# Moving the second quarter's sets of batch 0 behind the first feature tile

## The chip, the core and the metric

The kernel runs on one core of a Trainium2 chip. The metric is the device time of one execution in microseconds (us), as the median of several runs. Times inside an execution come from a hardware profile of one of them, counted from the start of its span.

The engines are TensorE (PE in the profile's rows; PEld is its weight loads), VectorE (DVE), ScalarE (ACT), GpSimd (POOL, which does nothing here) and SyncE (SP), which issues the loads from memory.

## The reference

Two things are computed in a row. First a two-way attention between 8 x 8 heads of 512 tokens and 32 state rows; then every row (tokens and state rows, 4608 of them with 512 columns) goes through a bilinear layer in float32:

```python
a = x @ w1            # 512 -> 1024
b = x @ w2
h = a * b @ w3        # 1024 -> 1024
return h @ w_out      # 1024 -> 512
```

The attention's token side is `softmax(x @ state.T / 8) @ state` per head, its state side is `softmax(state @ x.T / 8) @ x`. The weights are float64 and reach the chip as their bits.

## The kernel before

**Algebra.** The kernel multiplies `w3 @ w_out` once (`w34`, kept as `wo`, split into a high and a low part). A token's attention output is its softmax row times the state, so for every batch the kernel multiplies the state into `w1` and `w2` first (the "sets", tiles `sw_hi` and `sw_lo`), and the softmax rows (`at_hi`, `at_lo`) are then multiplied with these sets. A product of float32 accuracy is three products of rounded parts (hi x hi, hi x lo, lo x hi).

**Feature tiles.** The 1024 hidden columns are 8 feature tiles of 128. `stage1(b, ft)` (called `stage1_sums` and `hidden`) does one: 12 TensorE instructions at line 344 into a PSUM buffer of two banks, a copy by ScalarE (L325), a product by VectorE (L326), and a split into `g_hi` (ScalarE, L99) and `g_lo` (VectorE, L100). There are three two-bank buffers (`ps_2`), shared by feature tiles and sets, each free again after its last reader. Single banks (`ps_o`, two of them) serve the `w34` products.

**Weights.** `w1` and `w2` come in eight pieces of 128 x 1024 (`convert_half(n)`, n = 0 to 7): piece 2q is quarter q of `w1`, piece 2q + 1 the same of `w2`. Converting float64 bits takes, for each piece, a load of 1 MB by SyncE (L116) into one of three `raw` buffers, two ScalarE activates (L120 for the high words, L130 for the low words into one of two `ulps` buffers), then on VectorE a shift (L134) and an add (L138) into `w_sb`. `to_f32` is a generator: the first `go` on it issues the load and the two activates, the second `go` the shift and the add; `run` issues all of it.

**Sets.** `sets(quarter)` makes the sets of one quarter of the hidden columns for batch 0: two units (`w1` and `w2`), each 16 TensorE instructions (L151) into a PSUM buffer, and a split by ScalarE (L99) and VectorE (L100). Quarter q needs pieces 2q and 2q + 1; feature tiles 2q and 2q + 1 read its columns. Quarters 2 and 3 are made together by `sw_steps(0)[2:]`, two units that need pieces 4 and 6, and 5 and 7.

**The last w3 column tiles.** `w34(i)` makes row block i of `wo`: 8 products, 16 TensorE instructions at L635, into a single bank; `finish(i)` splits it into `wo` (L99, L100). `w34(7)` was cut in two: products 0 to 4 (`LAST = 5`) ahead of `sets(1)`, 5 to 7 behind it.

**What sets the order.** TensorE and SyncE run in the order written, throughout. ScalarE and VectorE do so in the prologue, until `order.close()` (L701). After it a planner orders their instructions by priority among those that it takes to be ready; it may also put such later instructions between or ahead of the written ones while those wait. `tc.high_priority()` in `hidden` raises a feature tile's evacuation. `tc.issue_after(ins)` keeps instructions of a block behind `ins` on its engine.

Around the change the order written is: `w34(6)`, `sets(0)`, `finish(6)`, five products of `w34(7)`, `sets(1)`, three products, `finish(7)`, end of the written order; then for quarter 0 feature tiles 0 and 1, the conversions of pieces 4 to 7, and batch 1's load (`load_x(1)`); for quarter 1 feature tile 2, `sw_steps(0)[2:]`, the first output products (`early_stage2(0)`, L358), feature tile 3, and so on.

Of the kernel before, what the change touches and what calls it, by code (L numbers as in the profile page):

```python
# [30 lines left out]
NF = 512  # L31
NW = 1024
AHEAD = 2
LAST = 5
PARTS = {0: (640, 1024), 1: (512, 1024)}
WARM = 15
PLAIN = 1
# [3 lines left out]
def attn_bilinear_kernel(  # L41
# [16 lines left out]
    FT, DO = w34_k.shape[0], out.shape[2]  # L58
    HALF = FT * P // NF
    QT = 2 * HALF  # L60
    NQ = NF // 2
# [28 lines left out]
    def bank():  # L90
        return ps_o.tile([P, NF], F32, name="ps_o")

    def two_banks():
        return ps_2.tile([P, 2, NF], F32, name="ps_2")

    def split(hi, lo, src):

        return (
            nc.scalar.copy(out=hi, in_=src),  # L99
            nc.vector.tensor_tensor(out=lo, in0=src, in1=hi.bitcast(F32), op=ALU.subtract),  # L100
        )
# [43 lines left out]
    def per_head(ps, b, moving):  # L145


        for j in range(NP):
            for q in range(KT):
                rows = slice(q * D, (q + 1) * D)  # L150
                nc.tensor.matmul(  # L151
                    ps[j * NS:(j + 1) * NS, q], sts[b][rows, j], moving(rows, j), start=True, stop=True
                )

    def load_x(b):
        sts[b] = att.tile([P, NP, NS], F32, name="st")
        nc.sync.dma_start(out=sts[b], in_=st[b])
        x_tiles[b] = att.tile([P, NP, S], F32, name="x_d", bufs=1)
        nc.sync.dma_start(out=x_tiles[b], in_=x_d[b])
# [132 lines left out]
        return scores, read_state, a2  # L292


    def sw_pair():
        return [main.tile([P, KT, NF], F32R, name=f"sw_{part}", bufs=2 * HALF) for part in ("hi", "lo")]

    def sw_steps(b):
        sw_tiles.setdefault(b, {})

        def unit(half, i):
            ps = two_banks()
            as_q = ps.rearrange("p k (c f) -> p k c f", c=2)
            per_head(as_q, b, lambda rows, j: w_sb[rows, 2 * half:2 * half + 2, i, j])
            sw_tiles[b][half, i] = sw_pair()
            split(*sw_tiles[b][half, i], ps)

        return [(lambda half=half, i=i: unit(half, i)) for half in range(HALF) for i in range(2)]

    def sw_quarter(b, quarter, i):  # L310
        tiles = sw_tiles.setdefault(b, {})
        half, c = divmod(quarter, 2)
        if c == 0:
            tiles[half, i] = sw_pair()
        ps = two_banks()[:, :, :NQ]
        per_head(ps, b, lambda rows, j: w_sb[rows, quarter, i, j])
        split(*(t[:, :, c * NQ:(c + 1) * NQ] for t in tiles[half, i]), ps)


    last_split, stored = [], []  # L320

    def hidden(ps, n, g_hi, g_lo):
        a_sb = main.tile([P, NF], F32, name="tmp", bufs=4)
        with tc.high_priority():
            nc.scalar.copy(out=a_sb[:, :n], in_=ps[:, 0, :n])  # L325
            nc.vector.tensor_tensor(out=a_sb[:, :n], in0=a_sb[:, :n], in1=ps[:, 1, :n], op=ALU.mult)  # L326
            last_split[:] = split(g_hi, g_lo, a_sb[:, :n])

    def new_g(ft):
        if ft < FT - 2:  # L330
            return [main.tile([P, NF], F32R, name=f"g_{part}", bufs=FT - 2) for part in ("hi", "lo")]
        both = main.tile([P, 2, NF], F32R, name="g_x", bufs=2)
        return [both[:, 0], both[:, 1]]

    def stage1_sums(b, ft):
        half, c = divmod(ft * P, NF)
        ps = two_banks()
        hi, lo = at_tiles[b]
        for i in range(2):
            w_hi, w_lo = sw_tiles[b][half, i]  # L340
            k = 0
            for kt in range(KT):
                for w, a in ((w_hi, lo), (w_hi, hi), (w_lo, hi)):
                    nc.tensor.matmul(  # L344
                        ps[:, i], w[:, kt, c:c + P], a[:, kt], start=(k == 0), stop=(k == 3 * KT - 1)
                    )
                    k += 1
        return ps

    def stage1(b, ft, gs):  # L350
        ps = stage1_sums(b, ft)
        gs.append(new_g(ft))
        hidden(ps, S, *gs[-1])
# [23 lines left out]
    def side_steps():  # L377

        scores, reads[1], _ = attention_steps(1)
        w = sw_steps(1)  # L380
        softmax, read = scores(), reads[0]()

        def rest():

            with tc.issue_after(stored[0].ins):
                yield from softmax
            yield from read

        loads = [partial(load_tokens, 1), partial(load_x, 2)]
        late_units[:] = w[3:]  # L390
        return [[partial(islice, softmax, 3)], [partial(islice, read, 1), *loads, *w[:3]], [rest], [], [], []]
# [4 lines left out]
    def combine_weights(k):  # L396

        raw = [tmp_tile() for _ in range(2)]
        for i, whole in enumerate(raw):
            nc.vector.tensor_tensor(  # L400
                out=whole, in0=wo["hi"][:, i * QF + k].bitcast(F32), in1=wo["lo"][:, i * QF + k].bitcast(F32), op=ALU.add
            )
        b11, b12, b21, b22 = (whole[:, half * HO:(half + 1) * HO] for whole in raw for half in range(2))
        t = late.tile([P, QF, S], F32, name="raw")[:, :, :HO]
        for j, (x, y) in enumerate(((b12, b11), (b22, t[:, 0]), (b22, b12), (b21, t[:, 1]))):
            nc.vector.tensor_tensor(out=t[:, j], in0=x, in1=y, op=ALU.subtract)
        yield
        split(t_parts["hi"][:, :, k], t_parts["lo"][:, :, k], t)
# [163 lines left out]
    def run(steps):  # L572
        for step in steps:
            for _ in step() or ():
                pass
# [11 lines left out]
    def finish(i):  # L587
        split(wo["hi"][:, i], wo["lo"][:, i], w34_ps[i][:, :DO])
# [7 lines left out]
    def split_of(k):  # L596

        def both():
            halves[k] = sw_pair()
            for n, src in enumerate((w_out[k], chunks[k][:, DO:])):  # L600
                split(*(t[:, n] for t in halves[k]), src)

        return both
# [27 lines left out]
    def w34(i, ks=range(FT)):  # L631
        if ks[0] == 0:
            w34_ps[i] = bank()
        for k in ks:
            nc.tensor.matmul(  # L635
                w34_ps[i][:, :DO], w3s[i][:, k * P:(k + 1) * P], w_out[k], start=(k == 0), stop=(k == FT - 1)
            )
# [5 lines left out]
    def sets(quarter):  # L643
        for i in range(2):
            sw_quarter(0, quarter, i)


    gs, acc, early = [], [], range(2)

    def early_stage2(quarter):  # L650
        if quarter == 0:
            acc.extend(bank() for _ in early)
        for ft in range(2 * quarter, 2 * quarter + 2):
            for tt in early:
                project(acc[tt], gs, tt, ft)
# [19 lines left out]
    go = lambda steps: next(steps, None)  # L675
# [18 lines left out]
    w34(6)  # L694
    sets(0)
    finish(6)
    w34(7, range(LAST))
    sets(1)
    w34(7, range(LAST, FT))
    finish(7)  # L700
    order.close()  # L701
    for quarter in range(QT):
        stage1(0, 2 * quarter, gs)
        if quarter == 1:
            run(sw_steps(0)[2:])
        if quarter:
            early_stage2(quarter - 1)
        if quarter == 1:
            side = side_steps()
            sums = combine_weights(0)  # L710
            go(sums)
        elif quarter == 2:
            run(side.pop(0))
        stage1(0, 2 * quarter + 1, gs)
        if quarter == 1:
            with tc.issue_after(last_split[0].ins), tc.issue_after(last_split[1].ins):
                go(sums)
        if quarter == 0:
            run([partial(convert_half, n) for n in range(4, 2 * QT)])
            load_x(1)  # L720
            prologue.close()
            late = ctx.enter_context(tc.tile_pool(name="late", bufs=1))
            t_both = late.tile([P, 4, QF, 2, HO], F32R, name="t")
            t_parts = {part: t_both[:, :, :, n] for n, part in enumerate(("hi", "lo"))}
            with tc.issue_after(last_split[1].ins):
                go(softmax)
# [91 lines left out]
```

## Time and profile before

| | us |
|---|---|
| median of 3 runs (488.54 to 489.65) | 488.63 |
| the profiled execution | 487.95 |
| its span | 486.2 |
| TensorE busy | 479.5 |
| VectorE busy | 393.4 |
| ScalarE busy | 237.6 |
| span until the first feature tile of batch 0 starts | 65.7 |

Busy time of an engine leaves out waits, branches and the issue of loads. Matmuls are pipelined and their ends are modelled. A bracket at the end of a row gives the idle time of the engine just before the instruction and what ended it. The granted TensorE clock was 1.00 throughout.

### The profile page before, as it was taken

The page shows a single profiled execution, that of the slowest core. Times are in us where ns is not written, and L with a number is a line of the kernel's source. Part 1 is how long each engine was busy: PE and PEld are TensorE (multiplying, and loading weights), DVE is VectorE, ACT ScalarE, POOL GpSimd, SP SyncE. Part 2 cuts the span into 40 slices and gives each one's busy share as a digit, 9 for nine tenths or more (in the row PEclk, how much of TensorE's full clock was granted, in tenths as well). Part 3 has the DMA queues.
Part 4 walks back from the last instruction along what each step waited for, and adds up shares of the span by engine and source line. Part 5 has one row for each costly group of instructions (what it writes and reads, how often), then busy time and mean ns, then how long its engine had stood idle before and what let it go on. Part 6 is the DMA issues. An engine that isn't in the chain of part 4 may idle for free.

```text
span 486.2 us, 8627 instructions
## 1 busy us (share of the span) xinstructions
PE 479.5 (99%) x3398; PEld 370.2 (76%) x3398; DVE 393.4 (81%) x580; ACT 237.6 (49%) x368; POOL 0.2 (0%) x4
## 2 busy tenths in 40 slices
PE   8999999999999999999999999999999999999996
PEld 5554467768788878887797779777977797899885
DVE  5778999798899589959985998599859985678870
ACT  4876984453547045605560555055515642353640
POOL 0000000000000000000000000000000000000000
PEclk9999999999999999999999999999999999999999
DMA  8996971163014404130413042304230223001101
GB/s 345 367 399 222 388 278 26 19 216 89 14 38 173 106 4 182 38 93 4 182 41 92 5 181 45 87 5 181 47 84 6 89 47 85 5 2 45 45 1 43
DMA packets 56361, 52.49 MB, mean 108 GB/s; under 512 B 42752, under 2 KB 50944, under 8 KB 51712
## 3 DMA queue, kind: packets, MB, share of 16 engines
q1 hardware_dynamic: 47488, 43.27, 26.8%
q10 hardware_dynamic: 8832, 8.65, 5.2%
q8 instruction: 27, 0.44, 0.4%
q14 instruction: 14, 0.11, 0.1%
HBM read 38.27 MB, written 8.91 MB: 97 GB/s over the span
## 4 chain that ended last, share of the span: by engine, by line
PE 93%; DVE 4%; ACT 1%; DMA 1%; issue 0%; DVEq 0%; ACTq 0%
PE ps L344 36%; PE ps_o L460 11%; PE ps L472 8%; PE ps L151 8%; PE ps_o L358 7%; PE ps_o L465 6%; PE ps L477 4%; PE ps L756 3%; PE ps_o L615 2%; PE ps L615 2%; PE ps_o L635 2%; PE ps L758 2%; PE ps_o L276 1%; DVE w_sb L138 1%; DMA raw<-in_w_k_dram 1%; PE ps L612 1%
## 5 line engine op out<-in xcount | busy, mean ns | idle before, releaser
L344 PE MATMUL ps<-at_lo,sw_hi 128*128 128x512 f32 x256 | 101.1, 395 | 0.0
L344 PE MATMUL ps<-at_hi,sw_hi 128*128 128x512 f32 x256 | 99.7, 389 | 0.0
L344 PE MATMUL ps<-at_hi,sw_lo 128*128 128x512 f32 x256 | 99.7, 389 | 0.0
L549 ACT COPY tmp<-ps 128x512 f32<-128x512 f32 x56 | 32.8, 585 | 121.5 <-PE ps L344 119.3
L344 PEld LDWEIGHTS ps<-at_lo,sw_hi 128*128 128x128 f32 x256 | 48.1, 188 | 15.9 <-DVE g_lo L100 4.2
L344 PEld LDWEIGHTS ps<-at_hi,sw_lo 128*128 128x128 f32 x256 | 48.1, 188 | 10.3
L344 PEld LDWEIGHTS ps<-at_hi,sw_hi 128*128 128x128 f32 x256 | 48.1, 188 | 9.5 <-issue 0.2
L488 DVE TENSOR_TENSOR tmp<-tmp,ps 128x512 f32<-128x512 f32 x42 | 28.9, 688 | 19.0 <-PE ps L477 18.1
L429 DVE TENSOR_TENSOR g_x<-tmp,ps 128x512 f32<-128x512 f32 x28 | 19.0, 679 | 26.4 <-ACT tmp L549 26.3
L100 DVE TENSOR_TENSOR sw_lo<-ps,sw_hi 128x1024 fp32r<-128x1024 f32 (+1 forms) x34 | 38.2, 1149 | 1.3 <-ACT sw_hi L99 1.3
L99 ACT CAST g_hi<-raw 128x512 fp32r<-128x512 f32 x42 | 24.6, 619 | 29.1 <-DVE raw L429 21.6
L151 PE MATMUL ps<-w_sb,st 64*32 64x512 f32 (+1 forms) x544 | 31.6, 570 | 0.4 <-DVE sw_lo L100 0.4
L99 ACT CAST sw_hi<-ps 128x1024 fp32r<-128x1024 f32 (+1 forms) x34 | 31.1, 969 | 1.8 <-PE ps L151 1.7
L460 PEld LDWEIGHTS ps_o<-t,g_hi 128*128 128x128 f32 x224 | 27.8, 191 | 5.0 <-issue 5.0
L99 ACT CAST g_hi<-g_x 128x512 fp32r<-128x512 f32 x42 | 25.6, 625 | 10.3 <-DVE g_x L429 5.3
L460 PE MATMUL ps_o<-t,g_hi 128*128 128x256 f32 x224 | 29.7, 286 | 0.0
L100 DVE TENSOR_TENSOR g_lo<-raw,g_hi 128x512 fp32r<-128x512 f32 x42 | 28.0, 681 | 1.6 <-PE ps_o L465 1.6
L460 PE MATMUL ps_o<-wo,g_hi 128*128 128x256 f32 x224 | 29.1, 283 | 0.0
L460 PEld LDWEIGHTS ps_o<-wo,g_hi 128*128 128x128 f32 x224 | 28.3, 192 | 0.5
L100 DVE TENSOR_TENSOR g_lo<-g_x,g_hi 128x512 fp32r<-128x512 f32 x42 | 27.2, 684 | 1.8 <-PE ps_o L465 1.8
L472 PE MATMUL ps<-t,g_hi 128*128 128x512 f32 x112 | 28.0, 392 | 0.0
L472 PEld LDWEIGHTS ps<-t,g_hi 128*128 128x128 f32 x112 | 20.2, 189 | 3.6
(125 smaller groups left out, 802.6 us busy)
## 6 DMA issues: line engine op xcount, KB each, us to landing
raw<-in_w_k_dram SPq DMA_DIRECT2D x8, 1024.0 KB, 6.0
x_d<-in_x_d_dram SPq DMA_DIRECT2D x8, 1024.0 KB, 7.4
raw<-in_w_dram SPq DMA_DIRECT2D x8, 1024.0 KB, 6.6
x_s<-in_x_s_dram SPq DMA_DIRECT2D x8, 1024.0 KB, 5.1
out_dram<-tmp ACTq DMA_DIRECT2D x56, 128.0 KB, 1.8
raw<-in_w3t_dram SPq DMA_DIRECT2D x4, 1024.0 KB, 7.0
e<-work SPq DMA_DIRECT2D x112, 32.0 KB, 2.0
sread<-turned SPq DMA_DIRECT2D x128, 4.0 KB, 1.7
```

The costliest lines, as they stand in the source:

```text
L99: nc.scalar.copy(out=hi, in_=src),
L100: nc.vector.tensor_tensor(out=lo, in0=src, in1=hi.bitcast(F32), op=ALU.subtract),
L151: nc.tensor.matmul(ps[j * NS:(j + 1) * NS, q], sts[b][rows, j], moving(rows, j), start=True, stop=True)
L344: nc.tensor.matmul(ps[:, i], w[:, kt, c:c + P], a[:, kt], start=(k == 0), stop=(k == 3 * KT - 1))
L358: nc.tensor.matmul(ps[:, :DO], g, wo[w][:, ft, :], start=(ft == 0 and k == 0), stop=(ft == FT - 1 and k == 2))
L460: nc.tensor.matmul(ps[:, tt * HO:(tt + 1) * HO], g, w(part, k), start=(fresh and k == 0 and tt == 0 and part == "lo"), stop=False, skip_gr ...
L465: nc.tensor.matmul(ps[:, tt * HO:(tt + 1) * HO], g, w("hi", k), start=False, stop=(k == QF - 1), skip_group_check=True)
L472: nc.tensor.matmul(ps[:, tt].rearrange("p (n d) -> p n d", n=2), g, w(k), start=(k == 0), stop=False, skip_group_check=True,)
L477: nc.tensor.matmul(ps[:, tt, :HO], g, w(k)[:, 0], start=False, stop=(k == QF - 1), skip_group_check=True)
L488: sum2 = lambda out, x, y: nc.vector.tensor_tensor(out=out, in0=x, in1=y, op=ALU.add)
L549: copied = nc.scalar.copy(out=a_sb, in_=ps[:, 0])
L615: nc.tensor.matmul(w34_ps[i][:, :DO], chunks[k][:, DO + i * P:DO + (i + 1) * P], w_out[k], start=(k == 0), stop=(k == FT - 1),)
```

## The change

Feature tile 0 and the sets of quarter 1 change places, and `w34(7)` is no longer cut around the sets: its eight products all stand ahead of feature tile 0. Pieces 4, 5 and 6 are no longer left to the planner but are issued at written places: the loads and activates of 4, 5 and 6 between the products of `w34(7)`, the shifts and adds of 4 and 5 ahead of feature tile 0, those of 6 behind `sets(1)`. Feature tile 0 itself now stands in the written order. `finish(7)` stays last. Piece 7 is still left to the planner, but its ScalarE and VectorE instructions may not be issued ahead of the last split of `sets(1)` (`parted`).

```diff
-LAST = 5
...
+    last_split, stored = [], []
...
-        split(*(t[:, :, c * NQ:(c + 1) * NQ] for t in tiles[half, i]), ps)
+        last_split[:] = split(*(t[:, :, c * NQ:(c + 1) * NQ] for t in tiles[half, i]), ps)
...
     finish(6)
-    w34(7, range(LAST))
+    w1_2, w2_2, w1_3 = map(convert_half, (4, 5, 6))
+    w34(7, range(2))
+    go(w1_2)
+    w34(7, range(2, 4))
+    go(w2_2)
+    w34(7, range(4, FT))
+    go(w1_3), go(w1_2), go(w2_2)
+    stage1(0, 0, gs)
     sets(1)
-    w34(7, range(LAST, FT))
+    parted = last_split[:]
+    go(w1_3)
     finish(7)
     order.close()
     for quarter in range(QT):
-        stage1(0, 2 * quarter, gs)
+        if quarter:
+            stage1(0, 2 * quarter, gs)
...
         if quarter == 0:
-            run([partial(convert_half, n) for n in range(4, 2 * QT)])
+            with tc.issue_after(parted[0].ins), tc.issue_after(parted[1].ins):
+                run([partial(convert_half, 7)])
             load_x(1)
```

More of the change, by code (lines that the diff above doesn't have):

```diff
@@ L316, in sw_quarter @@
         per_head(ps, b, lambda rows, j: w_sb[rows, quarter, i, j])
-        split(*(t[:, :, c * NQ:(c + 1) * NQ] for t in tiles[half, i]), ps)
-    last_split, stored = [], []
+        last_split[:] = split(*(t[:, :, c * NQ:(c + 1) * NQ] for t in tiles[half, i]), ps)
     def hidden(ps, n, g_hi, g_lo):
```

## The prediction

> **What bounds the kernel now.** I read the page first, then busy time by stretches, the waits of TensorE, the chain that ended last, and last the order of each engine between 56 and 85 us, where the edit lies.
>
> ```profile
> PE 479.5 (99%) x3398; PEld 370.2 (76%) x3398; DVE 393.4 (81%) x580; ACT 237.6 (49%) x368; POOL 0.2 (0%) x4
> ```
>
> ```profile
> 62.00:64.00 2.00, 1.59 (x34) 0.55 (x19) 2.00 (x5) 1.01 (x2) 0.00 (x0) 1.00 0.93 381
> ```
>
> ```profile
> 220.00:280.00 60.00, 60.00 (x505) 48.37 (x494) 52.01 (x77) 28.13 (x48) 0.00 (x0) 1.00 0.22 66
> ```
>
> ```profile
> PE ps L151 <- DVE sw_lo L100: 0.4, 1, 0.4
> ```
>
> TensorE is busy for 99% of the span. The only hole near the edit is 0.41 us in the stretch 62 to 64 (1.59 of 2.00), and later stretches such as 220 to 280 have none, so a shift of TensorE's work at 75 us is carried to the end unchanged. The hole belongs to the second unit of `sets(1)` (L151), which waits for VectorE. The chain shows the same place and what follows:
>
> ```profile
> 62.15 0.61 DVE sw_lo L100
> 62.76 0.04 issue
> 62.80 0.67 PE ps L151 x16
> 63.47 2.77 PE ps_o L635 x6
> 66.24 8.20 PE ps L344 x36
> 74.44 1.88 PE ps L151 x32
> ...
> 79.27 5.44 PE ps L344 x24
> ```
>
> Up to 62.8 us the chain is VectorE's; from there it is TensorE alone: six products of the last w3 column tile, three feature tiles (8.20 / 3 = 2.73 each), then the two whole-half units of `sw_steps` (L151, 32 instructions; the second starts half way, at 74.44 + 0.94 = 75.38). But VectorE is not idle beside it. It is busy without a break and has to finish piece 7 before that second unit:
>
> ```profile
> 58.24 0.69 DVE L134 TENSOR_SCALAR w_sb<-w_sb 128x1024 int32<-128x1024 int32 x1
> 58.96 1.22 DVE L138 CUSTOM_DVE_ANT_0 w_sb<-w_sb,ulps 128x2048 uint16<-128x2048 uint16 x1
> 60.10 0.69 DVE L134 TENSOR_SCALAR w_sb<-w_sb 128x1024 int32<-128x1024 int32 x1
> ...
> 62.06 1.28 DVE L100 TENSOR_TENSOR sw_lo<-ps,sw_hi 128x512 fp32r<-128x512 f32 x2
> 63.26 0.68 DVE L100 TENSOR_TENSOR wo<-ps_o,wo 128x512 fp32r<-128x512 f32 x1
> ...
> 69.73 0.68 DVE L326 TENSOR_TENSOR tmp<-tmp,ps 128x512 f32<-128x512 f32 x1
> 70.32 1.22 DVE L138 CUSTOM_DVE_ANT_0 w_sb<-w_sb,ulps 128x2048 uint16<-128x2048 uint16 x1
> 71.46 0.69 DVE L134 TENSOR_SCALAR w_sb<-w_sb 128x1024 int32<-128x1024 int32 x1
> ...
> 72.66 1.22 DVE L138 CUSTOM_DVE_ANT_0 w_sb<-w_sb,ulps 128x2048 uint16<-128x2048 uint16 x1
> ...
> 82.64 0.69 DVE L326 TENSOR_TENSOR tmp<-tmp,ps 128x512 f32<-128x512 f32 x1 [0.19 <-ACT tmp L325]
> 84.02 0.69 DVE L100 TENSOR_TENSOR g_lo<-tmp,g_hi 128x512 fp32r<-128x512 f32 x1 [0.69 <-ACT g_hi L99]
> ```
>
> From start to start, a shift takes 0.72 when its own add follows, an add 1.14, a 512-wide subtract or multiply 0.60. Piece 7's add ends at 72.66 + 1.22 = 73.88, which leaves 75.38 - 73.88 = 1.5 us of slack before TensorE needs it. That slack is what the edit spends. The last row shows the other thing to know: when the product and the `g_lo` of one feature tile stand next to each other on VectorE, it idles 0.69 us while ScalarE makes `g_hi`.
>
> [...] The stretch from 220 to 280 without a hole bears out the reading taken here, but only as long as the modelled ends hold.
>
> **The change, part by part.** Nothing is computed that was not before; four sequences move.
>
> *TensorE.* The order becomes: all eight products of column tile 7, feature tile 0, `sets(1)`, feature tile 1. Before:
>
> ```profile
> 57.25 4.56 PE L635 MATMUL ps_o<-w_sb,sw_lo 128*128 128x512 f32 x10
> 61.73 0.66 PE L151 MATMUL ps<-w_sb,st 64*32 64x256 f32 x16
> 62.80 0.67 PE L151 MATMUL ps<-w_sb,st 64*32 64x256 f32 x16 [0.41 <-DVE sw_lo L100]
> 63.40 2.84 PE L635 MATMUL ps_o<-w_sb,sw_lo 128*128 128x512 f32 x6
> ```
>
> ```profile
> 60.36 0.19 PEld L635 LDWEIGHTS ps_o<-w_sb,sw_lo 128*128 128x128 f32 x1 [0.24 <-issue]
> 60.78 0.19 PEld L635 LDWEIGHTS ps_o<-w_sb,sw_lo 128*128 128x128 f32 x1 [0.24 <-issue]
> ...
> 65.65 0.19 PEld L344 LDWEIGHTS ps<-at_lo,sw_hi 128*128 128x128 f32 x1 [0.24 <-issue]
> ```
>
> Loads of this tile come every 0.43 us. The tenth is at 60.78, so feature tile 0 loads at 60.78 + 7 x 0.43 = 63.79 in place of 65.65, 1.86 earlier. Its inputs are there: the second `sw_lo` of `sets(0)` ends at 62.06 + 1.28 = 63.34. Its end moves from 66.24 + 2.73 = 68.97 to 67.11. The 0.41 wait is gone, because `sets(1)` now comes 5 us later than both buffers that it needs.
>
> *The PSUM buffers.* There are three two-bank buffers. `sets(0)` holds two, feature tile 0 takes the third, `sets(1)` the two first. So feature tile 1 needs the one of feature tile 0, which is free only after its copy (ScalarE) and its product (VectorE). `sets(1)` covers 32 instructions, 0.60 to 0.67 per 16 by the rows, so TensorE could go on at about 67.0 + 1.2 = 68.2.
>
> *ScalarE.* Pieces 4, 5 and 6 are now written out ahead of feature tile 0, two activates each, so all six stand ahead of its copy. Before:
>
> ```profile
> 59.56 1.20 ACT L120 ACTIVATE w_sb<-raw 128x1024 f32<-128x1024 f32 x1
> 60.63 1.17 ACT L130 ACTIVATE ulps<-raw 128x1024 int32<-128x1024 uint32 x1
> ...
> 63.57 0.59 ACT L99 CAST sw_hi<-ps 128x512 fp32r<-128x512 f32 x1 [0.48 <-PE ps L151]
> 64.06 1.19 ACT L120 ACTIVATE w_sb<-raw 128x1024 f32<-128x1024 f32 x1
> 65.15 1.13 ACT L130 ACTIVATE ulps<-raw 128x1024 int32<-128x1024 uint32 x1
> ...
> 82.02 0.59 ACT L325 COPY tmp<-ps 128x512 f32<-128x512 f32 x1 [3.75 <-PE ps L344]
> ```
>
> ```profile
> raw<-in_w_dram SPq DMA_DIRECT2D x1, 1024.0 KB, 7.7
> ```
>
> ```profile
> raw<-in_w_dram SPq DMA_DIRECT2D x1, 1024.0 KB, 6.7
> ```
>
> ```profile
> 54.71 7.44 SPq L116 DMA_DIRECT2D raw<-in_w_dram  x3
> ```
>
> ```profile
> 58.27 3.88 SPq L116 DMA_DIRECT2D raw<-in_w_dram  x2
> ```
>
> The rows of time to landing are those of the loads issued at 51.76 (piece 4, 7.7 us) and 58.27 (piece 6, 6.7 us). SyncE's order of loads does not change: pieces 4 to 7, then batch 1's. Each waits for a raw buffer that ScalarE frees as before (piece 7 at 61.8, when piece 4's second activate ends), so I cost it at nothing. Piece 4 keeps its place at 59.56. Piece 5 takes about 61.9 to 64.0. Piece 6 lands at 58.27 + 6.7 = 64.97, its activates start at 65.0 and 66.07; the second also needs one of two `ulps` buffers, free when piece 4's add ends (65.8, next part). ScalarE is free at 67.15, and feature tile 0 ends at 67.11: the copy starts at **67.15**, with no margin left.
>
> *VectorE.* After `wo` at 63.26: piece 4's shift 63.86, add 64.58 to 65.80, piece 5's shift 65.72, add 66.44, free at 67.58. Then, in written order, feature tile 0's product 0.62 after its copy (82.02 to 82.64), so at 67.77, ending 68.46. Feature tile 1 goes on at **68.50** on TensorE, 0.3 later than it could. Against 68.62 before (65.65 + 0.43 + 11 x 0.23, the load of its first weights) that is 0.1 earlier: -0.41 for the wait removed, +0.3 for the new one. `g_lo` follows 1.38 after the product (82.64 to 84.02), at 69.15, with 0.69 + 0.09 idle ahead of it in this place; before, adds of pieces 6 and 7 filled it. Then `sets(1)`: 69.75 and 70.35; piece 6: shift 70.95, add 71.67; `wo` of tile 7 at 72.81; feature tile 1's product (its copy is done near 72.1) 73.41; piece 7: shift 74.0, add 74.7 to **75.95**.
>
> *What it comes to.* TensorE would reach the second `sw_steps` unit at 75.38 - 0.1 = 75.28. It needs piece 7 and the buffer of feature tile 1, both behind VectorE: 75.95 + 0.04 = 75.99. That is 75.99 - 75.38 = **+0.6 us**. Unknown is the order that the planner gives what is not written out. Without `wo` or the product ahead of piece 7, it ends 0.6 earlier, and the change costs 0.0; with `g_lo` of feature tile 1 ahead as well, 0.5 later, +1.1. If all waits vanished the end would be -0.41. I take +0.6, since `wo` is written ahead of piece 7 and the second unit needs the product anyway. Other users of late VectorE work have cover: VectorE has its first idle time only at 82.6 us, but the next feature tile that reads the `sw_steps` results starts at 79.27 + 2.72 = 82.0, and the results would be split by 81.
>
> Sum: the profiled run took 487.95 us, 486.2 of it span. 487.95 + 0.6 = 488.55; it lies 0.68 under the median of 488.63, so for the median 488.63 + 0.6 = **489.2**.
>
> **The rivals.**
>
> *The DVE gaps are hidden.* If piece 7 is in time, only -0.1 to -0.4 remains: 488.4. For it: 1.5 us of slack today. Against it: 0.96 us of gaps and at least 0.6 of feature tile 1 ahead of it use that up.
>
> *Piece 7 is queued behind `g_lo` of feature tile 1 too*: +1.1, 489.7. For it: feature work has priority where it is ready. Against: `g_hi` is ready only as piece 7's add could start.
>
> *Slower: the copy is stuck behind piece 6's load.* Before, no feature copy stood behind a load. Each microsecond that piece 6 lands after 65.0 delays its two activates, the copy, the product, feature tile 1 on TensorE and all that VectorE does after, piece 7 at the end. With the 7.7 us of piece 4's load it lands at 65.97, the second unit starts at 77.0: +1.6, 490.2. It decides from a landing 0.9 us late on (above +1.47). Against it: the requests ahead of it in the loads' queue are unchanged. [...]
>
> *Faster beyond noise.* The only wait there is to win is 0.41 us, and no later stretch has a hole to close, so a gain of 1.5 us (487.1) has no source but a luckier later order.
>
> **How the numbers follow.** A measurement of this kernel can tell 0.3%, 1.47 us, from no change. Chances: forecast (0.0 to +0.9) 0.47; hidden gaps 0.18; `g_lo` ahead 0.11; late load, or a still later piece 7, 0.17; faster 0.07. The first three lie within 0.3%: 0.76. The range goes from -0.7 (all waits gone, and 0.3 of spread between runs) to +1.7 (the slow rival): 487.9 to 490.3.
>
> **What would show it.** Right: no wait before the second `sets(1)` unit; a wait of about 0.3 before feature tile 1 for `tmp` (L326); VectorE idle about 0.7 ahead of the first `g_lo`; a wait of 0.3 to 1.0 at `sw_steps` for L138; the later stretches unchanged. Wrong: no wait at `sw_steps` (then hidden gaps), ScalarE waiting for `raw` ahead of the copy beyond 67.2 (then the slow rival), or holes after 100 us.

## The result, and the profile after

| | us |
|---|---|
| median after, 6 runs (491.39 to 492.89) | 492.03 |
| median before, 6 runs beside them (488.44 to 489.83) | 488.61 |
| ratio, 95% interval | 1.0063 [1.0051, 1.0076] |
| the profiled execution after, its span | 492.27, 490.5 |

The change makes the kernel 3.4 us slower. The forecast was 489.2 with a range of 487.9 to 490.3: the sign was right, the size was not, and the result lies outside the range. The engines' row of the page shows the same work as before: TensorE 479.5, VectorE 393.6.

```profile
PE 479.5 (98%) x3398; PEld 369.7 (75%) x3398; DVE 393.6 (80%) x580; ACT 237.3 (48%) x368; POOL 0.2 (0%) x4
```

TensorE's busy time is the same to 0.1 us, so the loss is waiting. From here on most line numbers are one smaller than before (L150 was L151, L137 was L138, L99 was L100). TensorE's waits from 55 to 110 us (total, times, longest):

```profile
PE ps L150 <- DVE w_sb L137: 2.2, 1, 2.2
PE ps L344 <- DVE tmp L326: 1.2, 1, 1.2
PE ps_o L635 <- DVE wo L99: 0.8, 1, 0.8
```

The first row is the second `sw_steps` unit waiting for piece 7's add, the second is feature tile 1 waiting for tile 0's product. Both waits were forecast, at 0.7 and 0.3. The 0.41 wait of the second `sets(1)` unit is gone, as forecast. So the edit costs 2.16 + 1.20 - 0.41 = **2.95 us**. The third row lies ahead of the edit, at 57 us, where the instructions are those of before: loads landed later in this execution, and all from there on stands 1.07 us later. That wait was 0.0 to 0.8 in the profiles of all kernels below. Nothing comes after the edit; the busy time by stretches (span, PE, PEld, DVE, ACT, POOL, clock, DMA share, GB/s) has no hole later:

```profile
220.00:280.00 60.00, 60.00 (x521) 47.44 (x520) 49.05 (x71) 26.12 (x45) 0.00 (x0) 1.00 0.22 69
```

The chain that ended last, where before TensorE alone stood from 62.8 us on:

```profile
59.32 7.52 DMA raw<-in_w_dram
...
66.92 1.15 ACT w_sb L119
68.08 1.09 ACT ulps L129
69.17 0.48 ACT tmp L325
...
69.68 0.70 DVE tmp L326
...
70.42 5.75 PE ps L344 x24
...
76.19 0.60 ACT tmp L325
...
76.81 0.69 DVE tmp L326
77.50 0.60 DVE wo L99
78.09 1.14 DVE w_sb L137
79.24 0.14 issue
79.37 1.09 PE ps L150 x16
```

It leaves TensorE twice. First: piece 6's load, its two activates, the copy of feature tile 0, its product, feature tile 1. Second, at 76.16, when feature tile 2 has just ended: the copy of **tile 2**, its product, `wo`, and only then piece 7's add. The second detour takes 79.37 - 76.16 = 3.21 us, of which only the first `sw_steps` unit covers about one. VectorE's own order shows it:

```profile
72.86 1.38 DVE L133 TENSOR_SCALAR w_sb<-w_sb 128x1024 int32<-128x1024 int32 x2
74.16 0.68 DVE L326 TENSOR_TENSOR tmp<-tmp,ps 128x512 f32<-128x512 f32 x1
74.75 1.22 DVE L137 CUSTOM_DVE_ANT_0 w_sb<-w_sb,ulps 128x2048 uint16<-128x2048 uint16 x1
75.89 0.68 DVE L99 TENSOR_TENSOR g_lo<-tmp,g_hi 128x512 fp32r<-128x512 f32 x1
76.81 0.69 DVE L326 TENSOR_TENSOR tmp<-tmp,ps 128x512 f32<-128x512 f32 x1 [0.23 <-ACT tmp L325]
77.41 0.68 DVE L99 TENSOR_TENSOR wo<-ps_o,wo 128x512 fp32r<-128x512 f32 x1
78.01 1.21 DVE L137 CUSTOM_DVE_ANT_0 w_sb<-w_sb,ulps 128x2048 uint16<-128x2048 uint16 x1
```

Both shifts are done by 74.2 (the first row, two instructions), and piece 7's second activate ends on ScalarE at 75.09, so the add could have stood at 75.9, right behind piece 6's. The planner instead puts tile 1's product, piece 6's add, `g_lo` of tile 1, tile 2's product and `wo` ahead of piece 7's add. ScalarE shows the first detour: it waits 1.75 for the load, and the copy of tile 0 stands behind both activates although TensorE had left the tile at 68.1 (`sets(1)` starts at 68.12).

```profile
66.92 1.15 ACT L119 ACTIVATE w_sb<-raw 128x1024 f32<-128x1024 f32 x1 [1.75 <-DMA raw<-in_w_dram]
67.98 1.19 ACT L129 ACTIVATE ulps<-raw 128x1024 int32<-128x1024 uint32 x1
69.06 0.58 ACT L325 COPY tmp<-ps 128x512 f32<-128x512 f32 x1
```

### The profile page after: what moved, and what is told of

Its sections match the earlier page's. It is cut to its first block, busy times and chain, and to the rows that moved or that the text cites. A ratio compares the mean times of both kernels' runs of the same rounds, so it can differ in the third digit from the quotient of the medians.

```text
span 490.5 us, 8629 instructions
## 1 busy us (share of the span) xinstructions
PE 479.5 (98%) x3398; PEld 369.7 (75%) x3398; DVE 393.6 (80%) x580; ACT 237.3 (48%) x368; POOL 0.2 (0%) x4
## 4 chain that ended last, share of the span: by engine, by line
PE 84%; DMA 6%; ACT 6%; DVE 3%; issue 0%; ACTq 0%; DVEq 0%
PE ps L344 35%; PE ps_o L460 11%; PE ps L472 8%; PE ps L150 7%; PE ps_o L358 7%; PE ps_o L465 5%; PE ps L477 4%; PE ps L766 3%; DMA raw<-in_w_k_dram 2%; DMA raw<-in_w3t_dram 2%; ACT ulps L129 2%; ACT w_sb L119 2%; PE ps L768 2%; DMA raw<-in_w_dram 2%; PE ps_o L275 1%; DVE w_sb L137 1%
## 5 line engine op out<-in xcount | busy, mean ns | idle before, releaser
L344 PE MATMUL ps<-at_lo,sw_hi 128*128 128x512 f32 x256 | 101.3, 396 | 1.2 <-DVE tmp L326 1.2
L344 PE MATMUL ps<-at_hi,sw_lo 128*128 128x512 f32 x256 | 99.8, 390 | 0.0
L344 PE MATMUL ps<-at_hi,sw_hi 128*128 128x512 f32 x256 | 99.7, 390 | 0.0
L344 PEld LDWEIGHTS ps<-at_lo,sw_hi 128*128 128x128 f32 x256 | 48.1, 188 | 17.7 <-DVE g_lo L99 4.2
L344 PEld LDWEIGHTS ps<-at_hi,sw_lo 128*128 128x128 f32 x256 | 48.0, 188 | 10.3
L344 PEld LDWEIGHTS ps<-at_hi,sw_hi 128*128 128x128 f32 x256 | 48.1, 188 | 9.5 <-issue 0.2
L99 DVE TENSOR_TENSOR sw_lo<-ps,sw_hi 128x1024 fp32r<-128x1024 f32 (+1 forms) x34 | 38.1, 1145 | 1.3 <-ACT sw_hi L98 1.3
L150 PE MATMUL ps<-w_sb,st 64*32 64x512 f32 (+1 forms) x544 | 31.6, 570 | 2.2 <-DVE w_sb L137 2.2
L99 DVE TENSOR_TENSOR g_lo<-raw,g_hi 128x512 fp32r<-128x512 f32 x42 | 27.9, 677 | 1.6 <-PE ps_o L465 1.6
L99 DVE TENSOR_TENSOR g_lo<-g_x,g_hi 128x512 fp32r<-128x512 f32 x42 | 27.1, 681 | 1.8 <-PE ps_o L465 1.8
L119 ACT ACTIVATE w_sb<-raw 128x1024 f32<-128x1024 f32 (+3 forms) x18 | 18.7, 1051 | 8.8 <-DMA raw<-in_w_k_dram 6.9
```

What stands on the lines that cost most here:

```text
L119: nc.scalar.activation(out=out[:, part], in_=high.bitcast(F32), func=AF.Prelu, scale=2.0**-112, alpha=-(2.0**32))
L150: nc.tensor.matmul(ps[j * NS:(j + 1) * NS, q], sts[b][rows, j], moving(rows, j), start=True, stop=True)
L344: nc.tensor.matmul(ps[:, i], w[:, kt, c:c + P], a[:, kt], start=(k == 0), stop=(k == 3 * KT - 1))
```

## The experiments

The theories that the expectations name: **A**, piece 7's add is passed by feature work on VectorE; **B**, the load of piece 6 holds ScalarE's copy of feature tile 0; **C**, the exchange of tile 0 and `sets(1)`, with its PSUM buffers, costs by itself; **D**, the granted clock falls after a long wait. E, G and W are variants, told where they appear. Each ratio is to the kernel before, run on the same chip beside it.

| kernel | median us (before beside it) | ratio, 95% | waits: tile 1; `sw_steps` | last add of pieces 6 and 7 behind tile 2's product |
|---|---|---|---|---|
| the change, run again | 493.04 (489.3) | 1.0073 [1.0051, 1.0096] | 0.9; 2.1 | yes |
| e1 | 493.69 (489.4) | 1.0100 [1.0080, 1.0119] | 1.0; 2.2 | yes |
| e2 | 493.5 (489.4) | 1.0094 [1.0076, 1.0112] | 0.4; 3.0 | yes |
| e9 | 492.66 (489.46) | 1.0074 [1.0049, 1.0098] | 0.8; 2.8 | yes, piece 6's |
| e10 | 492.92 (489.46) | 1.0084 [1.0055, 1.0113] | 0.4; 3.1 | yes |
| e3 | 491.05 (489.4) | 1.0041 [1.0026, 1.0055] | 0.4; 1.0 | no |
| e6 | 490.95 (489.05) | 1.0033 [1.0018, 1.0048] | 0.4; 1.4 | no |
| e5 | 490.34 (489.3) | 1.0025 [1.0012, 1.0038] | 1.1; 0.2 | no |
| e7 | 490.11 (489.3) | 1.0014 [1.0000, 1.0028] | 0.9; 0 | no |
| e4 | 489.59 (489.4) | 1.0012 [1.0001, 1.0022] | 0.4; 0.4 | no |
| e8 | 488.98 (489.3) | 1.0001 [0.9988, 1.0013] | 0.4; 0.4 | no |

(For e7, without the exchange, the first wait is feature tile 1's for the split of `sets(1)`.) The table is sorted by its last column, which turned out to decide.

**e4: TensorE's new order alone.** Kernel before; pieces 4 to 7 stay with the planner.

```diff
-    w34(7, range(LAST))
+    w34(7)
+    stage1(0, 0, gs)
     sets(1)
-    w34(7, range(LAST, FT))
...
-        stage1(0, 2 * quarter, gs)
+        if quarter:
+            stage1(0, 2 * quarter, gs)
```

> The kernel before with TensorE's new order alone: column tile 7 in one piece, feature tile 0, then sets(1), all in the written order; pieces 4 to 7 stay with the planner as before. Theories A and B (where the pieces were written costs): the planner fills the gaps with the pieces, 488.4 to 489.2. Theory C (the order of TensorE with three PSUM buffers costs): 491 to 492, with a wait of about 1 us ahead of feature tile 1.

Measured 1.0012 [1.0001, 1.0022]: the exchange costs some 0.6 us, at most 1.1. Its two waits, 0.4 each, take the place of the 0.41 that went:

```profile
PE ps L344 <- DVE tmp L326: 0.4, 1, 0.4
PE ps L151 <- DVE w_sb L138: 0.4, 1, 0.4
```

The time lies 0.4 over what A and B expected and far under what C did: C falls as the cause of 3.4 us.

**e8: the exchange, with pieces 4 and 5 written and 6 and 7 given back to the planner.**

```diff
-    w1_2, w2_2, w1_3 = map(convert_half, (4, 5, 6))
+    w1_2, w2_2 = map(convert_half, (4, 5))
...
-    go(w1_3), go(w1_2), go(w2_2)
+    go(w1_2), go(w2_2)
...
-    go(w1_3)
...
-            with tc.issue_after(parted[0].ins), tc.issue_after(parted[1].ins):
-                run([partial(convert_half, 7)])
+            run([partial(convert_half, n) for n in (6, 7)])
```

> The changed kernel with the exchange, pieces 4 and 5 written as in the change, pieces 6 and 7 left to the planner without a gate. Theories A and B: piece 6's shift fills the gap ahead of g_lo, no copy stands behind a load, the wait at sw_steps falls to about 0.5, 489.5 to 490.2. Theory C: as the changed kernel.

Ratio 1.0001: the whole loss is gone, more than A and B expected (489.5 to 490.2 against 488.98). VectorE's order now has the add of piece 7 (74.47) ahead of tile 2's product (76.21):

```profile
73.64 0.68 DVE L326 TENSOR_TENSOR tmp<-tmp,ps 128x512 f32<-128x512 f32 x1
74.47 1.23 DVE L137 CUSTOM_DVE_ANT_0 w_sb<-w_sb,ulps 128x2048 uint16<-128x2048 uint16 x1
75.61 0.68 DVE L99 TENSOR_TENSOR g_lo<-tmp,g_hi 128x512 fp32r<-128x512 f32 x1
76.21 0.68 DVE L326 TENSOR_TENSOR tmp<-tmp,ps 128x512 f32<-128x512 f32 x1
```

So the loss needs what the change does with pieces 6 and 7; the exchange alone does not bring it.

**e9 and e10: the two corners between.** e9 is the change with only the hold on piece 7 removed; e10 is the change with only piece 6 given back, so that both pieces stand behind the last split of `sets(1)`.

```diff
 (e9)
-    parted = last_split[:]
...
-            with tc.issue_after(parted[0].ins), tc.issue_after(parted[1].ins):
-                run([partial(convert_half, 7)])
+            run([partial(convert_half, 7)])
```

```diff
 (e10; piece 6's three written steps go as in e8)
             with tc.issue_after(parted[0].ins), tc.issue_after(parted[1].ins):
-                run([partial(convert_half, 7)])
+                run([partial(convert_half, n) for n in (6, 7)])
```

> The changed kernel with only the hold on piece 7 taken away (it is left to the planner from the end of the written order on, as in the kernel before); piece 6 stays written ahead of feature tile 0. If the hold on piece 7 is what puts its add behind feature work (theory G), the wait at sw_steps falls under 0.6 and the time to 490.0 to 490.6, leaving only the wait of about 1.1 before feature tile 1. If the written piece 6 alone delays all that VectorE does (theory W), piece 7's add still stands behind tile 2's product and the wait at sw_steps stays 1.0 to 2.2: 491.2 to 492.5.

> The changed kernel with only piece 6 given back to the planner; both it and piece 7 are held behind the last split of sets(1). Theory W (the written piece 6 alone is the cause): the copy of feature tile 0 is free, the wait before feature tile 1 falls to 0.4 and piece 7 comes in time, 489.0 to 489.6. Theory G (the hold costs): the two pieces can only start their shifts after 71 us, the first product of wo @ w_out, tile 2's product and g_lo of tile 1 pass the add of piece 7, the wait at sw_steps is 1.8 to 2.8: 491.0 to 492.5.

Each alone brings the whole loss: 1.0074 and 1.0084, with only e8, which takes both away, free of it. So the two causes don't add. W foresaw the loss in e9 and G the one in e10, both a little low (492.5 at most), and each missed the other run. VectorE, ScalarE and TensorE in e9:

```profile
69.30 0.69 DVE L133 TENSOR_SCALAR w_sb<-w_sb 128x1024 int32<-128x1024 int32 x1 [0.34 <-ACT w_sb L119]
...
73.89 1.22 DVE L137 CUSTOM_DVE_ANT_0 w_sb<-w_sb,ulps 128x2048 uint16<-128x2048 uint16 x1
...
75.63 0.68 DVE L326 TENSOR_TENSOR tmp<-tmp,ps 128x512 f32<-128x512 f32 x1
76.23 1.22 DVE L137 CUSTOM_DVE_ANT_0 w_sb<-w_sb,ulps 128x2048 uint16<-128x2048 uint16 x1
```

```profile
68.11 1.15 ACT L119 ACTIVATE w_sb<-raw 128x1024 f32<-128x1024 f32 x1
...
72.55 1.14 ACT L129 ACTIVATE ulps<-raw 128x1024 int32<-128x1024 uint32 x1
```

```profile
77.59 3.33 PE L150 MATMUL ps<-w_sb,st 64*32 64x512 f32 x32 [2.84 <-DVE w_sb L137]
```

Here it is piece 6's add that comes last, not piece 7's. Piece 6's activates have ended by 67.8; the two shown are piece 7's. VectorE's shift at 69.30 waited for the first of them, and the add at 73.89 follows the end of the second (73.69): without the hold, piece 7's shift and add have gone ahead, and the add at 76.23, behind tile 2's product, is piece 6's. That is why already the first `sw_steps` unit stands still: it needs pieces 4 and 6. So W, which had piece 7's add last here, was right about the time and not about the order. VectorE and ScalarE in e10:

```profile
75.75 0.69 DVE L326 TENSOR_TENSOR tmp<-tmp,ps 128x512 f32<-128x512 f32 x1
76.36 0.68 DVE L99 TENSOR_TENSOR g_lo<-tmp,g_hi 128x512 fp32r<-128x512 f32 x1
76.96 1.22 DVE L137 CUSTOM_DVE_ANT_0 w_sb<-w_sb,ulps 128x2048 uint16<-128x2048 uint16 x1
```

```profile
74.03 1.22 ACT L129 ACTIVATE ulps<-raw 128x1024 int32<-128x1024 uint32 x1
75.15 0.57 ACT L325 COPY tmp<-ps 128x512 f32<-128x512 f32 x1
```

In e10 it is piece 7's add again, and two things make its wait of 3.07. Piece 7's activates come late: the second ends at 75.25, as the first `sw_steps` unit does. And from there the add is passed by tile 2's product and `g_lo` and starts 1.7 later, at 76.96; its own length does the rest.

What tile 2's product waits for differs. In the profile after, in e1 and in the change run again, its copy waits for TensorE to end tile 2 (ScalarE stands idle for 0.58, 0.15 and 0.58 ahead of it), so the add behind it hangs on TensorE's own work. In e10 and e2 the copy stands behind piece 7's second activate instead.

**e2: piece 6's load and activates behind `sets(1)`.**

```diff
-    go(w1_3), go(w1_2), go(w2_2)
+    go(w1_2), go(w2_2)
     stage1(0, 0, gs)
     sets(1)
...
+    go(w1_3)
```

> The changed kernel, but piece 6's load and activates are written behind sets(1) in place of ahead of feature tile 0, so that no copy of a feature tile stands behind them on ScalarE. Theory B: the wait of 1.2 us ahead of feature tile 1 falls to about 0.3, all behind it moves up by 0.9, 491.1. Theory A: the wait ahead of feature tile 1 falls as well, but piece 7's add still stands last and the wait at sw_steps grows by what was saved, 491.7 to 492.0. Theory C: the wait ahead of feature tile 1 stays near 1 us, 492.0.

The wait before tile 1 fell to 0.4, so B is right about that wait. The time did not fall, and 493.5 is above what any theory gave (492.0 at most): piece 7's activates, behind those of piece 6, now end at 76.19, its add stands behind tile 2's product here too, and the wait at `sw_steps` rose to 3.0.

**e1: piece 7 in the written order, ahead of the split of `wo`.**

```diff
-    w1_2, w2_2, w1_3 = map(convert_half, (4, 5, 6))
+    w1_2, w2_2, w1_3, w2_3 = map(convert_half, (4, 5, 6, 7))
...
-    go(w1_3)
+    go(w2_3), go(w1_3), go(w2_3)
...
-            with tc.issue_after(parted[0].ins), tc.issue_after(parted[1].ins):
-                run([partial(convert_half, 7)])
```

> The changed kernel, but piece 7 also stands in the written order: its load and activates behind the last split of sets(1), its shift and add behind piece 6's and ahead of the split of column tile 7. Theory A (the planner's order: piece 7's add stood behind the g_lo of feature tile 1, the product of tile 2 and wo, and TensorE waited 2.16 us for it): its add ends near 76.7 on the changed kernel's clock, the wait at the sw_steps unit falls to 0.2 or less, 490.0 us. Theory B (the late load of piece 6 holds ScalarE's copy of feature tile 0, and everything behind is late for that reason): the wait at sw_steps shrinks by at most 0.4, 491.6. Theory C (the order of sets and feature tile itself costs, by the PSUM buffers): 492.0.

Missed: 1.0100. Writing piece 7 first doesn't keep its add there. While an add waits for its own shift the planner fills in what it takes to be ready, and by now that is feature work:

```profile
75.69 0.69 DVE L133 TENSOR_SCALAR w_sb<-w_sb 128x1024 int32<-128x1024 int32 x1
76.29 0.68 DVE L400 TENSOR_TENSOR tmp<-wo 128x512 f32<-128x512 f32 x1
77.20 0.69 DVE L326 TENSOR_TENSOR tmp<-tmp,ps 128x512 f32<-128x512 f32 x1 [0.23 <-ACT tmp L325]
77.81 0.68 DVE L99 TENSOR_TENSOR g_lo<-tmp,g_hi 128x512 fp32r<-128x512 f32 x1
78.41 1.22 DVE L137 CUSTOM_DVE_ANT_0 w_sb<-w_sb,ulps 128x2048 uint16<-128x2048 uint16 x1
```

The wait at `sw_steps` stayed 2.2, so the run could not test A yet.

**e3: both edits together.** Piece 6's load and activates behind `sets(1)` as in e2, piece 7 written as in e1.

> Both of the edits: piece 6's load and activates behind sets(1), and piece 7 in the written order ahead of the split of column tile 7. Theories A and B together: waits of 0.3 ahead of feature tile 1 and at most 0.3 at sw_steps are left, 489.0. A alone: 490.0. B alone: 491.1. C: 491 to 492, the waits stay.

1.0041, waits 0.4 and 0.8 + 0.2; A and B together expected 489.0, and 491.05 is near the figure given for B alone (491.1). Here the add is ahead of tile 2's product, but the activates of both pieces come late: the add starts at 76.33, as soon as the second one ends (76.31).

**e5: the add held ahead by force.** e1, and the products and `g_lo` of tiles 1 and 2 and the first `wo` combine step may not be issued on VectorE before piece 7's add (`seventh`).

```diff
...
+    seventh = last_add[0].ins
...
-            stage1(0, 2 * quarter, gs)
+            with tc.issue_after(seventh) if quarter == 1 else ExitStack():
+                stage1(0, 2 * quarter, gs)
...
-            go(sums)
+            with tc.issue_after(seventh):
+                go(sums)
...
-        stage1(0, 2 * quarter + 1, gs)
+        with tc.issue_after(seventh) if quarter == 0 else ExitStack():
+            stage1(0, 2 * quarter + 1, gs)
```

> Piece 7 in the written order and, on VectorE, the products and g_lo of feature tiles 1 and 2 and the first step of combine_weights held behind piece 7's add. So its add cannot be passed as it was in the first experiment. Theory A: the add ends about 3.8 us behind piece 6's shift, the wait at sw_steps is 0.3 or less, no clock drop: 2.0 us under the changed kernel on this chip. Theory B alone: at most 0.5 under it. Theory C: as the changed kernel.

```profile
PE ps L346 <- DVE tmp L328: 1.1, 1, 1.1
...
PE ps L152 <- DVE tmp L328: 0.2, 1, 0.2
```

```profile
75.16 1.23 DVE L139 CUSTOM_DVE_ANT_0 w_sb<-w_sb,ulps 128x2048 uint16<-128x2048 uint16 x1
76.30 1.28 DVE L328 TENSOR_TENSOR tmp<-tmp,ps 128x512 f32<-128x512 f32 x2
```

(L346, L152, L139 and L328 are L344, L150, L137 and L326 there.) Piece 7's add now stands ahead of both products. e5 differs from e1 by the hold alone, and 1.0100 has become 1.0025, so the order on VectorE decides. 490.34 stands against 493.04 for the change beside it: of these 2.7 us the wait at `sw_steps`, which goes from 2.1 to 0.2, is 1.9; beside the rest stands the granted clock, 0.50 from 79.5 to 82.0 us in the profile of the change run again and 1.00 there in that of e5. A is shown. What stays is the 1.1 before tile 1.

**e6: e5 with piece 6 behind `sets(1)`.** It takes both suspected causes away; E, its rival, says that what is won before tile 1 is lost again.

> The changed kernel with both suspected causes taken away: piece 7's add placed ahead of the later feature work on VectorE (as in the kernel with the order held), and piece 6's load and activates written behind sets(1), so that ScalarE's copy of feature tile 0 no longer stands behind a load. Theory A plus B (the order of piece 7's add, and the copy behind piece 6's load, are all of the loss): the wait before feature tile 1 falls from 1.1 to 0.4, the wait at sw_steps stays under 0.6 (piece 7 is then bound by its own activates, which come later); time 488.9 to 489.8, 0.5 to 1.0 below the kernel with the order held alone (490.34). Rival E: what is won before feature tile 1 is lost again at sw_steps, because piece 6 moved later pushes piece 7's activates later: wait at sw_steps 0.8 to 1.2, time 490.0 to 491.

E: 1.0033, not less than e5's 1.0025. The wait before tile 1 fell to 0.4, that at `sw_steps` rose to 1.4. Piece 7's two activates now come last on ScalarE; the add waits for the second and starts at 75.11, and tile 1's product, held behind it, ends at 76.95, where the second `sw_steps` unit gets its buffer:

```profile
73.93 1.15 ACT L131 ACTIVATE ulps<-raw 128x1024 int32<-128x1024 uint32 x1
```

So two activates (2.1 us of ScalarE from start to start) ahead of the copy delay tile 1, and behind it they delay piece 7. The way out in e8 is finer than either: its planner puts one activate of piece 6 right behind the copy, and the other behind the splits of `sets(1)`.

**e7: the change without the exchange.** `sets(1)` stands ahead of feature tile 0 again; pieces 4 to 6 stay written, 7 held.

```diff
-    stage1(0, 0, gs)
     sets(1)
...
-        if quarter:
-            stage1(0, 2 * quarter, gs)
+        stage1(0, 2 * quarter, gs)
```

> The changed kernel without the exchange: sets(1) stand ahead of feature tile 0 again, behind all eight products of column tile 7; pieces 4 to 6 stay written where the change puts them, piece 7 gated. Theories A and B (the written pieces and the planner's treatment of piece 7 cost, not the exchange): 491 to 492.5, with a wait at sw_steps of 1 us or more. Theory C (the exchange costs): 489 to 489.6.

1.0014, between the forecasts (491 to 492.5 by A and B, 489 to 489.6 by C; 490.11 measured), with one wait:

```profile
PE ps L344 <- DVE sw_lo L99: 0.9, 1, 0.9
```

Without the exchange ScalarE still waits 1.7 us for the load of the written piece 6; it is the split of `sets(1)` that stands behind it. But piece 7's add comes at 75.70, ahead of tile 2's product at 76.83. So the written pieces cost some 0.7 us alone, the exchange some 0.6 alone, and both together 3.1 to 3.6: what goes beyond the sum comes with the order that only the two together give VectorE.

**The change run again**, beside e5, e7 and e8.

> The changed kernel again, beside the next three. A (order), B (late load) and C all expect its ratio of 1.006 to 1.010 again. Beside them D: where the wait at sw_steps leaves TensorE idle for 2 us or more, the granted clock may fall to 0.5 for about 3 us behind it, as the first experiment's profile shows from 80.3 to 83.6 us; so runs of 494 and above should be those with a mean clock under 0.998.

1.0073, with waits of 0.9 and 2.1, as in the first profile.

**Six and seven products ahead of `sets(1)` in the kernel before** (`LAST = 6`, `LAST = 7`): can the 0.41 wait be had without the rest?

> The kernel before with six in place of five products of the last column tile ahead of sets(1), nothing else. If the 0.41 us wait of the second unit of sets(1) is all that there is to win here, one product (0.43 us) more ahead of it covers it: 488.2 to 488.4 against 488.6, a ratio of 0.9992, no wait at that place. If the wait moves to another place (feature tile 0, or the buffers of sw_steps), no change.

> The kernel before with seven products ahead of sets(1): the wait has a cover of 0.86 us in place of 0.41, so it is gone also where VectorE comes 0.4 us late. Time as with six: 488.2 to 488.4. If the later split of sets(1) delays feature tile 1's buffer or piece 7's add on VectorE, a wait of 0.2 to 0.5 before feature tile 1 or at sw_steps and 488.6 to 489.

No: 0.9997 [0.9985, 1.0008] and 1.0009 [0.9997, 1.0020]. The wait at `sets(1)` is gone in both, but at 102 us a new one of the same size stands; the row of six:

```profile
102.10 1.95 PE L151 MATMUL ps<-w_sb,st 64*32 64x512 f32 x32 [0.42 <-DVE tmp L326]
```

No kernel of this study is faster than the kernel before.

## Why the prediction was wrong

- **TensorE** held: the 0.41 wait is gone, feature tile 0 starts at 63.8 (64.88 less the 1.07 of this execution), `sets(1)` behind it finds its buffers free (by the forecast's own numbers 3.7 us after `sets(0)`'s last split, not 5), no later stretch has a hole, and the shift of 75 us went to the end.
- **ScalarE** was forecast at a copy of tile 0 at 67.15 "with no margin left"; it was at 69.06, which is 67.99 without the 1.07. The landing of piece 6 was mis-sized: 7.52 after the issue where the profile before had 6.7. That is the slow rival's mechanism, and its threshold (0.9 late) was just not reached (0.82). The copy is 0.84 later than forecast, and the wait before tile 1 was 1.2 instead of 0.3. In the three ScalarE rows of the profile after the ready copy did not pass the two activates: TensorE had left tile 0 at 68.1, and the copy started at 69.06.
- **What it comes to** is the step that failed. It had piece 7's add behind `wo` and tile 1's product, ending at 75.95, and bounded the planner's freedom at +1.1 by `g_lo` of tile 1. In the trace `g_lo` of tile 1 and **tile 2's product** stood ahead of it too. Tile 2's product cannot start before TensorE has ended tile 2, so in this order the slack of 1.5 us, counted from the earlier edge, stopped mattering: the wait is the copy, product, `wo` and add behind tile 2, 3.21 us, less the first unit. I bounded a queue by adding operations to it (0.6 each), and never asked which of them waits for the engine that I was timing. Where the wait was forecast at 0.7, it was 2.16.
- The sum -0.41 + 0.3 + 0.7 = +0.6 became -0.41 + 1.20 + 2.16 = +2.95. The rivals "`g_lo` ahead" and "copy stuck" were each held to be alone; both happened, and the first went further than its bound.
- The rest of the 3.4 us between the medians goes with the granted clock. Of the twelve timed executions of the change, the six with a mean clock of 0.997 took 492.44 to 494.53, the six with 0.998 to 1.000 took 491.39 to 492.27. Of the six in the first table, the four at 0.998 or above have a median of 491.7, 3.0 us above the kernel before and close to the 2.95 of waits; the last section has the profiles in which the clock fell.
- One size on VectorE was read too small: the shifts of pieces 4 and 5 start 0.82 ahead of their adds, not 0.72. It cost nothing, since VectorE then waited 0.74 for the copy.
- The idle 0.69 us ahead of the first `g_lo` (71.05) came as forecast, and hidden gaps (488.4) fell: the forecast was right that the slack would be used up.

## What to carry to other kernels

When a consumer waits for a queue whose order a planner picks, bound the wait by the latest *input* that anything placed ahead may wait for, not by adding up durations; if that input is the waiting engine's own last result, starting earlier should not hide the wait (this follows from the order in the profile after; no run here isolates it). Writing one step out by hand (piece 6) or holding one back (piece 7) moves all that the planner fits around it: either alone cost the whole loss here, though not by the same piece, and leaving both to it cost nothing. So establish which piece comes last in each run before naming the cause. A load's landing read from one profile is not a constant of the next kernel (piece 6's took 6.7 us before, 7.5 after); where a ready instruction is written behind it on one engine, as the copy of tile 0 was here, ask what 1 us more would do.

## What the runs showed of the hardware

**The granted clock fell to half for 3.4 us at four of the six TensorE waits of over 2 us at `sw_steps`.** Two stretches of e1, behind its 2.21 us wait that ended at 79.78:

```profile
80.00:82.00 2.00, 2.00 (x18) 0.80 (x3) 2.00 (x4) 0.78 (x1) 0.00 (x0) 0.61 0.00 0
82.00:84.00 2.00, 2.00 (x6) 1.52 (x6) 2.00 (x2) 0.23 (x1) 0.00 (x0) 0.54 0.10 16
```

The column ahead of the last two is the clock; the two shortfalls, 0.39 and 0.46 of 2 us, make 3.4 us at half. In the chain the 12 instructions at L358 then took 4.22 us instead of 2.94, and the unit before 1.40 instead of 1.09, together +1.6. The profiles of e9 (wait 2.84), e10 (3.07) and the change run again (2.15) show it too, each with the clock at 0.50 in five or more half-microsecond stretches on end and a shortfall of 1.7 us in all; those of the change (2.16) and e2 (3.0) don't, with 1.00 in every such stretch from 72 to 86 us. The other nine, with waits of at most 1.4 between 55 and 110 us, have 1.00 from 57 to 110. So D is a cost on top that comes with the long wait, not a cause of it.

The length of the wait alone doesn't decide: 2.15 us (the change run again) came with the fall, 2.16 (the change) and 3.0 (e2) without it. Nor does the fall start where the wait ends: TensorE goes on at 79.78 in e1 and the clock is still 1.00 up to 80.0; in e10 it goes on at 78.33, and the stretch from 78.0 to 78.5 already has 0.68. What else decides, these runs don't show.

**A load's landing moved with an edit that doesn't touch loads.** Piece 6's load took 6.6 to 6.7 us from issue to landing in the profiles of the kernel before and of six and seven products, where `w34(7)` is cut around `sets(1)`. It took 7.2 to 7.6 in all twelve profiles of kernels with `w34(7)` in one piece, e4 and e7 among them, though SyncE issues the same loads in the same order. The loads of pieces 4 and 5 agree (7.6 to 7.7, and 7.1) in the profiles before, after, of e4 and of seven products. What holds the later one isn't settled.
